# Attention inside a fused kernel, from the third batch on: four heads to a piece, score products on 64 array rows

## The chip, the cores and the metric

The kernel runs on one core of a Trainium2 chip. Its engines are TensorE (PE in the profile; PEld is its loading of stationary operands), VectorE (DVE), ScalarE (ACT), GpSimd (POOL) and the queue engine SyncE (SP). The metric is the device time of one execution in microseconds, lower is better.

## The reference

Masked attention over 8 batches, 8 heads, 576 positions and 64 values per head, followed by a gated two-layer network over all 4608 positions. All of it is float32.

```
scores = q @ k.T / sqrt(64)            # per batch and head
heads 0-3: keep 0 <= q_pos - k_pos < 32
heads 4-7: keep k_pos <= q_pos with k_pos % 32 == q_pos % 32
attn = softmax(where(kept, scores, -1e9));  x = attn @ v
x -> [4608, 512]                       # 8 heads side by side
h = x @ w_in                           # [512, 2048]
out = (h * erf(softplus(h))) @ w_out   # [2048, 512]
```

The masks are so sparse that a block of 96 (local heads) or 126 (strided heads, positions sorted by remainder) queries needs only 128 or 126 keys.

## The kernel before

**The network** is 192 slots: 12 chunks of 384 positions by 16 tiles of 128 hidden values. A slot is a first product `mm1` of 12 matmuls (line 457, tile `h` in PSUM, three buffers), a chain of ten steps that alternates between ACT and DVE and computes the gate (lines 465, 462, 492, 495, 498; the DVE step on line 492 is the last reader of `h` and so frees its buffer), and a second product `mm2` of nine matmuls (line 527) into three accumulators `o`. Each float32 factor is split into a high and a low part, hence three products each.

**Attention** works in pieces. A piece is one batch `b`, one pair of heads `hp` (0 and 1 local, 2 and 3 strided) and one third `j` of the positions. Local pieces have two blocks of 96 queries by two heads; strided ones two blocks of 126 (`j` 0 and 1) or one of 72 (`j` 2). The steps of a piece, for batches 2 to 7:

- `scores` on PE (line 261): per block one matmul. The stationary operand is 128 keys, with the 64 values of one head on array rows 0 to 63 and those of the other on rows 64 to 127. The moving operand is block diagonal: the queries of head 0 with zeros below, then those of head 1 with zeros above, so 192, 252 or 144 columns of which each is half zero.
- `mask` on DVE (line 282) adds the mask and moves the scores from PSUM to SBUF, `maxi` on POOL (line 287) takes the maximum over partitions, `sub` on DVE (line 296) subtracts it, `exp` on ACT (line 300).
- `av` on PE (line 304): per block and head one matmul with the probabilities as the stationary operand and 65 moving columns (the 65th of ones gives the sum). Then sum, reciprocal and scaling on DVE, `transp` on PE (line 335), and a split into `xhi` (ACT) and `xlo` (DVE), from which `mm1` reads.

A float32 matmul of the program appears as two weight loads and two matmul rows in the trace; a transpose as one.

Batches 0 and 1 run ahead of and into the first slots, with the mask added by PE. Attention for a later pair of batches runs among the slots of the pair before.

**What sets the order.** A planner (`Plan`) holds all steps with an assumed duration, a key and their inputs, and lays them out by list scheduling: on each engine, of what can start soonest, the lowest key. A step that opens a buffer waits until the last reader of the buffer it replaces. The result is written out engine by engine, and the engines run it in that order. Attention shares two PSUM buffers, `ps`, among score tiles, `av` tiles and transposes; SBUF buffers are two for `qk`, `mx`, `xn` and `r`, and three for `sm` and `v`.

Of the kernel before, what the change touches and what calls it, by code (L numbers as in the profile page):

```python
# [8 lines left out]
F32 = mybir.dt.float32  # L9
# [3 lines left out]
AF = mybir.ActivationFunctionType  # L13
ALU = mybir.AluOpType

B, H, S, D = 8, 8, 576, 64
DM, DF = 512, 2048
NT = B * S
P = 128
# [9 lines left out]
PRO, SLOT = 78.281, 5.385  # L29
# [4 lines left out]
A0K, A0S, A0D = 6.648, 4.179, -9.111  # L34
A1K, A1S, A1D = PRO - 0.655, 3.9, 5.799
ASH, ADT = -0.644, 1.759
# [3 lines left out]
QL = 96  # L40
RB = 7
NA = S // 32
QS = RB * NA
WL = 2 * 2 * QL + 2 * QL + 32
WS = 2 * 2 * QS + 2 * P
# [43 lines left out]
class Plan:  # L89
# [13 lines left out]
    def add(self, eng, dur, key, emit, after=(), new=(), use=(), earliest=0.0):  # L103
        op = Op(eng, dur, key, emit, after, new, use, earliest)
        self.ops.append(op)
        return op

    def _ready(self, op, live):
        t = op.earliest
        for p in op.after:  # L110
            if p.end is None:
                return None
            t = max(t, p.end + (self.SAME if p.eng == op.eng else self.LATENCY)[op.eng])
        for b in op.new:
            order = live.setdefault(b.tag, [])
            n = len(order) - self.bufs[b.tag]
            if n >= 0:
                for u in order[n].users:
                    if u.end is None:
                        return None  # L120
                    t = max(t, u.end + (self.SAME if u.eng == op.eng else self.LATENCY)[op.eng])
        return t
# [46 lines left out]
def attention_moe(  # L169
# [10 lines left out]
    nc = tc.nc  # L180
# [3 lines left out]
    apool = ctx.enter_context(tc.tile_pool(name="apool", bufs=2))  # L184
    mpool = ctx.enter_context(tc.tile_pool(name="mpool", bufs=2))
    wpool = ctx.enter_context(tc.tile_pool(name="wpool", bufs=1))
    ps_a = ctx.enter_context(tc.tile_pool(name="ps_a", bufs=2, space=PSUM))
# [3 lines left out]
    xhi = [cpool.tile([P, RING], F32R, name=f"xhi{c}") for c in range(NCC)]  # L191
    xlo = [cpool.tile([P, RING], F32R, name=f"xlo{c}") for c in range(NCC)]
    ident = cpool.tile([P, P], F32, name="ident")
    con = cpool.tile([P, NCON], BF16, name="con")
    mask_l = con[:, : 2 * QL].rearrange("p (b h q) -> p b h q", b=2, h=1)
    mask_s = con[:, 2 * QL : 2 * QL + QS].rearrange("p (u q) -> p u q", u=1)
# [7 lines left out]
    plan = Plan(bufs)  # L204
    pools = {"apool": apool, "mpool": mpool, "wpool": wpool, "ps_a": ps_a, "ps_h": ps_h, "ps_o": ps_o}

    def buf(pool, tag, shape, name, dtype=F32):
        def make():
            return pools[pool].tile(shape, dtype, tag=tag, name=name, bufs=bufs[tag])

        return Buf(tag, make)

    def dve(n, x=1.0):
        return 0.067 + n * x / 960.0

    def act(n, fixed=0.093):
        return fixed + n / 1200.0


    def piece(b, hp, j, key, dt, ring, pe_mask=False, pool_sub=False, early=False):  # L220
# [4 lines left out]
        loc = hp < 2  # L225
        nblk = 1 if (not loc and j == 2) else 2
        n = QL if loc else (QS if j < 2 else S - 4 * QS)
        units, cols = 2 * nblk, 2 * nblk * n
        pid = f"{b}_{hp}_{j}"
        qk = buf("apool", "qk", [P, WS], f"qk_{pid}")  # L230
        v = buf("apool", "v", [P, 2, 2, D + 1], f"v_{pid}")
        s = buf("ps_h", "h", [P, 512], f"s_{pid}") if early else buf("ps_a", "ps", [P, 512], f"s_{pid}")
        sm = buf("apool", "sm", [P, 4 * QS], f"sm_{pid}")
        mx = buf("apool", "mx", [P, 4 * QS], f"mx_{pid}")
        pav = buf("ps_o", f"o{hp % 2}", [P, 512], f"av_{pid}") if early else buf("ps_a", "ps", [P, 512], f"av_{pid}")
        xn = buf("apool", "xn", [P, 4, D], f"xn_{pid}")
        rc = buf("apool", "r", [P, 4, 1], f"r_{pid}")
        pt = buf("ps_a", "ps", [P, 512], f"t_{pid}")
# [121 lines left out]
        add = plan.add  # L360
        w = nblk * n
        lq = add("sp", P * 4 * (WL if loc else nblk * (2 * n + P)) / 3.6e5, key - 8.0, load_qk, new=[qk])
        lv = add("sp", P * 4 * nblk * 2 * (D + 1) / 3.6e5, key - 7.9, load_v, new=[v])
        per = max(2 * n / 600.0, 0.213) + (2 * n / 2400.0 if pe_mask else 0.0)
        o_s = add("pe", 0.02 + nblk * per, key, scores, [lq, *o_con], [s, sm], [qk])
# [11 lines left out]
        o_e = add("act", act(cols), key + dt + 0.1, exp, [o_b], [], [sm, s] if early else [sm])  # L377
        o_v = add("pe", 0.00174*n * units, key + dt + 0.2, av, [o_e, lv], [pav, xn], [sm, v])
        o_r = add("dve", 0.07, key + 1.5 * dt, total, [o_v], [rc], [pav])
        o_r = add("dve", 0.1, key + 1.5 * dt, invert, [o_r], [], [rc])  # L380
        if early:
            o_n = add("act", 0.2 * units, key + 1.5 * dt + 0.1, norm, [o_r], [], [pav, xn, rc])
        else:
            o_n = add("dve", dve(units * D), key + 1.5 * dt + 0.1, norm, [o_r], [], [pav, xn, rc])
        o_t = add("pe", 0.11 * nblk, key + 2 * dt, transp, [o_n] + ring, [pt], [xn])
        o_h = add("act", act(w, 0.06), key + 2 * dt + 0.1, split_hi, [o_t], [], [pt])
        return [add("dve", dve(w), key + 2 * dt + 0.2, split_lo_x, [o_h], [], [pt])]


    def weight(i, src, rows, sl, key):  # L390
# [175 lines left out]
    o = plan.add("sp", 0.6, -20.0, load_consts, new=[con_f])  # L566
    o_con = [plan.add("dve", 0.6, -19.0, copy_consts, [o], [], [con_f])]
# [3 lines left out]
    x_of = {}  # L571
# [3 lines left out]
    for f in range(0, DF, SW):  # L575
        for c in range(NCC):
            i = len(w1)
            rows, sl = slice(c * P, (c + 1) * P), slice(f, f + SW)
            op, pair = weight(i, w_in, rows, sl, W1K[i // 4] + W1S[i // 4] * (i % 4))
            w1.append(op)  # L580
            win.append(pair)
    for f in range(NFC):
        rows, sl = slice(f * P, (f + 1) * P), slice(0, DM)
        op, pair = weight(NFC + f, w_out, rows, sl, W2K + W2S * f)
# [3 lines left out]
    def order(b):  # L588
        if b % 2:
            return [(hp, j) for j in range(3) for hp in (0, 2, 1, 3)]  # L590
        if b == 0:
            return [(0, 0), (1, 0), (0, 1), (1, 1), (2, 0), (3, 0), (2, 1), (3, 1), (2, 2), (3, 2), (0, 2), (1, 2)]
        return [(hp, j) for j in range(2) for hp in range(2)] + [
            (2, 0), (3, 0), (0, 2), (2, 1), (3, 1), (1, 2), (2, 2), (3, 2)
        ]

    def chunk(c):
        need = [o for b in (2 * (c // 3), 2 * (c // 3) + 1) for o in x_of.get((b, c % 3), [])]
        for f in range(NFC):
            k = c * NFC + f  # L600
            ready = (need + w1[4 * (f // 4) : 4 * (f // 4) + 4], [w2[f]])
            mm1_of[k], _ = ftile(k, ready)
            mm1_first.append(mm1_of[k])

    for b in range(B):
        p2 = b // 2
        for i, (hp, j) in enumerate(order(b)):

            if b % 2 == 0:
                to = [0] if (hp < 2 and j < 2) else ([1] if hp < 2 else [0, 1])  # L610
            else:
                to = [1] if (hp < 2 and j == 0) else ([2] if hp < 2 else [1, 2])
            if b == 0:
                key, dt = A0K + A0S * i, A0D
            elif b == 1:
                key, dt = A1K + A1S * i, A1D
            else:
                if b % 2:
                    slot = 48 * p2 - 3 + (15 * i) / 11
                elif i < 4:  # L620
                    slot = 48 * (p2 - 1) + 13 + 4 * i
                else:
                    slot = 48 * (p2 - 1) + 29 + (15 * (i - 4)) / 7
                key, dt = PRO + SLOT * (slot + ASH), ADT * SLOT
            ring = []
            if p2:
                ring = [mm1_of[48 * (p2 - 1) + 16 * c + 15] for c in to]
            done = piece(b, hp, j, key, dt, ring, pe_mask=b < 2, pool_sub=False, early=b == 0)
            for c in to:
                x_of.setdefault((b, c), []).extend(done)  # L630
        if b % 2 == 0:
            continue
        for c in range(3 * p2, 3 * p2 + 3):
            chunk(c)
# [109 lines left out]
```

## Time and profile before

| | |
|---|---|
| median of 3 runs | 994.1 us (993.43 to 994.18) |
| profiled execution | 993.13 us |
| its span in the trace | 991.2 us |
| PE busy | 979.5 us, 99% of the span |
| DVE, ACT, POOL busy | 74%, 66%, 15% |

The span leaves 1.93 us of the execution outside the trace. The duration of a PE row covers a matmul from its first reading to its modelled end, and rows overlap; so what a stretch costs is read from the start of one row to the start of the next, which is what the chain of waits prints.

### The profile page before, as it was taken

What the parts mean: (1) busy time and instruction counts of PE and PEld (TensorE: products, weight loads), DVE (VectorE), ACT (ScalarE), POOL (GpSimd) and SP (SyncE); (2) the same over time, 40 slices, a digit from 0 to 9 for tenths busy, and PEclk for the clock granted to TensorE, in tenths of its full rate; (3) what the DMA queues carried; (4) which work ended last, traced back from release to release, by engine and by line L of the source; (5) the groups of instructions that cost most, each with busy time, mean ns of one, the idle gap of its engine ahead of it and who ended that gap; (6) DMA issues with size and microseconds to landing.
All of it is one profiled execution on the core that took longest, in us unless ns stands there. A gap on an engine that the chain in (4) does not pass through costs nothing.

```text
span 991.2 us, 15250 instructions
## 1 busy us (share of the span) xinstructions
PE 979.5 (99%) x5443; PEld 885.6 (89%) x5443; DVE 728.7 (74%) x1619; ACT 654.7 (66%) x1481; POOL 152.8 (15%) x100
## 2 busy tenths in 40 slices
PE   8999999999999999999999999999999999999998
PEld 6788999999899989999899999999899999999997
DVE  6999997677677776676777776776767776665664
ACT  4676777567566666666765665766766576766765
POOL 3534111111112110011112110111111210000000
PEclk9999999999999999999999999999999999999999
DMA  9994211111222211111222220211112220000000
GB/s 310 308 338 144 63 35 59 40 40 53 71 62 82 62 37 38 46 53 27 80 58 73 71 63 19 70 40 40 49 53 66 63 63 1 32 2 0 32 1 33
DMA packets 37659, 68.76 MB, mean 69 GB/s; under 512 B 4176, under 2 KB 18640, under 8 KB 37584
## 3 DMA queue, kind: packets, MB, share of 16 engines
q1 hardware_dynamic: 37584, 67.80, 22.1%
q8 instruction: 43, 0.70, 0.3%
q14 instruction: 32, 0.26, 0.1%
HBM read 58.34 MB, written 9.44 MB: 68 GB/s over the span
## 4 chain that ended last, share of the span: by engine, by line
PE 91%; DVE 8%; ACT 0%; issue 0%; DMA 0%
PE h L457 39%; PE o L527 39%; PE s L261 5%; PE av L304 5%; DVE w L415 1%; PE t L335 1%; DVE w L421 1%; DVE pair L429 1%; DVE a L462 1%; DVE w L408 1%; DVE glo L498 1%; DVE b L492 0%; DVE xlo L358 0%; DVE b L462 0%; PE warm L638 0%
## 5 line engine op out<-in xcount | busy, mean ns | idle before, releaser
L527 PE MATMUL o<-pair,ghi 128*128 128x512 f32 x1152 | 372.3, 404 | 0.0
L457 PE MATMUL h<-xhi,pair 128*128 128x384 f32 x1536 | 306.7, 341 | 1.4 <-DVE b L492 1.4
L457 PEld LDWEIGHTS h<-xhi,pair 128*128 128x128 f32 x1536 | 271.9, 188 | 15.7 <-DVE b L492 3.8
L465 ACT ACTIVATE b<-b 128x384 f32<-128x384 f32 x384 | 199.7, 521 | 104.2 <-DVE b L462 101.6
L287 POOL PARTITION_ALL_REDUCE mx<-sm x96 | 152.6, 1594 | 664.1 <-DVE sm L282 568.7
L527 PEld LDWEIGHTS o<-pair,ghi 128*128 128x128 f32 x1152 | 207.0, 188 | 28.0
L527 PE MATMUL o<-pair,glo 128*128 128x512 f32 x576 | 225.9, 392 | 0.0
L457 PE MATMUL h<-xlo,pair 128*128 128x384 f32 x768 | 165.9, 337 | 0.0
L498 DVE TENSOR_TENSOR glo<-b,ghi 128x384 fp32r<-128x384 f32 x192 | 110.5, 576 | 60.3 <-ACT ghi L495 59.8
L462 DVE SCALAR_TENSOR_TENSOR a<-h,a 128x384 f32<-128x384 f32 x192 | 106.4, 554 | 64.9 <-ACT a L465 63.3
L457 PEld LDWEIGHTS h<-xlo,pair 128*128 128x128 f32 x768 | 137.2, 187 | 0.0
L462 DVE SCALAR_TENSOR_TENSOR a<-a,h 128x384 f32<-128x384 f32 x192 | 105.5, 549 | 40.7 <-ACT b L465 38.6
L465 ACT ACTIVATE b<-a 128x384 f32<-128x384 f32 x192 | 100.5, 524 | 47.6 <-DVE glo L498 47.1
L527 PEld LDWEIGHTS o<-pair,glo 128*128 128x128 f32 x576 | 108.1, 188 | 24.1
L495 ACT CAST ghi<-b 128x384 fp32r<-128x384 f32 x192 | 97.9, 510 | 46.8 <-PE o L527 41.6
L492 DVE TENSOR_TENSOR b<-b,h 128x384 f32<-128x384 f32 x192 | 105.1, 547 | 31.2 <-ACT b L465 30.9
L465 ACT ACTIVATE a<-a 128x384 f32<-128x384 f32 x192 | 100.2, 522 | 26.6 <-DVE a L462 24.3
L465 ACT ACTIVATE a<-h 128x384 f32<-128x384 f32 x192 | 92.7, 483 | 33.4 <-PE h L457 32.3
L462 DVE SCALAR_TENSOR_TENSOR b<-b,a 128x384 f32<-128x384 f32 x192 | 110.5, 576 | 3.2
L304 PEld LDWEIGHTS av<-v,sm 128*96 128x96 f32 (+2 forms) x704 | 78.0, 171 | 7.8 <-ACT sm L300 1.5
L261 PE MATMUL s<-qk 128*128 128x192 f32 (+2 forms) x352 | 83.4, 351 | 0.1
L304 PE MATMUL av<-v,sm 128*96 128x65 f32 (+2 forms) x704 | 77.9, 251 | 1.1 <-ACT sm L279 0.7
(34 smaller groups left out, 588.4 us busy)
## 6 DMA issues: line engine op xcount, KB each, us to landing
qk<-qk_loc SPq DMA_DIRECT2D x48, 304.0 KB, 2.8
qk<-qk_str SPq DMA_DIRECT2D x32, 380.0 KB, 3.2
v<-v_all SPq DMA_DIRECT2D x80, 130.0 KB, 2.1
out<-ob SPq DMA_DIRECT2D x36, 256.0 KB, 2.1
words<-w_in SPq DMA_DIRECT2D x16, 512.0 KB, 5.6
words<-w_out SPq DMA_DIRECT2D x16, 512.0 KB, 5.9
qk<-qk_str SPq DMA_DIRECT2D x16, 136.0 KB, 2.1
v<-v_all SPq DMA_DIRECT2D x16, 65.0 KB, 1.9
```

Source lines behind the costliest of these rows:

```text
L261: yield nc.tensor.matmul(dst, qk[:, k0 + blk * step : k0 + blk * step + P], qk[:, blk * 2 * n : (blk + 1) * 2 * n], start=blk == 0, stop=n ...
L287: yield nc.gpsimd.partition_all_reduce(mx[:, :cols], sm[:, :cols], P, ReduceOp.max)
L304: yield nc.tensor.matmul(pav[:n, u * (D + 1) : (u + 1) * (D + 1)], sm[:, u * n : (u + 1) * n], v[:, u // 2, u % 2, :], start=True, stop=True,)
L335: yield nc.tensor.transpose(pt[:, blk * n : (blk + 1) * n], xn[:n, 2 * blk : 2 * blk + 2, :].rearrange("p h d -> p (h d)"), ident[:n, :n],)
L408: yield nc.vector.tensor_scalar(out=w.tile.bitcast(U32), in0=words[:, :, 1], scalar1=0x07FFFFFF, scalar2=3, op0=ALU.bitwise_and, op1=ALU.l ...
L457: yield nc.tensor.matmul(ph[:, :CH], win[4 * s + cc][:, w, fs], x[cc][:, c0 : c0 + CH], start=(i == 0), stop=(i == len(terms) - 1))
L462: yield nc.vector.scalar_tensor_tensor(out=out, in0=in0, scalar=scalar, in1=in1, op0=op0, op1=op1)
L465: yield nc.scalar.activation(dst, src, func, bias=bias[i], scale=scale)
L492: yield nc.vector.tensor_tensor(out=bb.tile, in0=bb.tile, in1=ph[:, :CH], op=ALU.mult)
L495: yield nc.scalar.copy(ghi.tile, bb.tile)
L498: yield nc.vector.tensor_tensor(out=glo.tile, in0=bb.tile, in1=ghi.tile.bitcast(F32), op=ALU.subtract)
L527: yield nc.tensor.matmul(po.tile, g[:, ts], wout[f][:, w], start=(f == 0 and i == 0), stop=(f == NFC - 1 and i == 2),)
```

## The change

From batch 2 on, `quad` takes the place of `piece`: both head pairs of a kind (hp 0 and 1, or 2 and 3) go through one set of steps. Six quads make a batch instead of twelve pieces. Of the planner, one line changes: a step that opens several buffers of one kind now waits for the last reader of as many old ones.

- `scores`: for two-block quads (`tiled`) the matmul of a block falls into one per head, each with 64 array rows and 96 or 126 moving columns without the zeros. All eight of a quad stand together; head 0 of each block goes to PSUM tile `s0`, head 1 to `s1`. The quad with one block keeps the block-diagonal form, four heads in one tile.
- `mask`, `maxi`, `sub`, `exp` work tile by tile: two of each per two-block quad, with as many columns as before (384 or 504); one of each with 288 columns for the one-block quad.
- `av` is one step of 16 (or 4) matmuls after both `exp`; transposes of both pairs go to one PSUM tile; the splits are unchanged.
- A two-block quad opens two `ps` tiles for scores and then two for `av`, so all that there are, and two of three `sm` buffers.

```diff
+        def place(i, blk, h):
+            if tiled:
+                return h, (2 * i + blk) * n
...
+        def scores():
+            k0, step = units * n, n if loc else P
+            used = set()
+            for i in range(2):
+                for blk in range(nblk):
+                    keys = slice(k0 + blk * step, k0 + blk * step + P)
+                    for h in range(2) if tiled else (slice(0, 2),):
+                        rows = slice(h * D, (h + 1) * D) if tiled else slice(0, P)
+                        bank, c = place(i, blk, h if tiled else 0)
+                        q0 = (blk * 2 + (h if tiled else 0)) * n
+                        width = n if tiled else 2 * n
+                        yield nc.tensor.matmul(
+                            s[bank][:, c : c + width], qk[i][rows, keys], qk[i][rows, q0 : q0 + width],
+                            start=bank not in used,
+                            stop=True, skip_group_check=True,
+                        )
+                        used.add(bank)
...
+        o_s = add("pe", d_s, key, scores, [*lq, *o_con], [*s, *sm], [*qk])
+        o_e = []
+        for k in range(nbank):
+            o = add("dve", dve(cols), key + 0.1 + 0.01 * k, mask(k), [o_s], [], [s[k], sm[k]])
+            o = add("pool", 0.4 + cols * 0.0028, key + 0.2 + 0.01 * k, maxi(k), [o], [mx[k]], [sm[k]], earliest=6.7)
+            o = add("dve", dve(cols), key + dt + 0.01 * k, sub(k), [o], [], [mx[k], sm[k]])
+            o_e.append(add("act", act(cols), key + dt + 0.1 + 0.01 * k, exp(k), [o], [], [sm[k]]))
+        o_v = add("pe", 0.00174 * n * 2 * units + 0.05, key + dt + 0.2, av, [*o_e, *lv], [*pav, *xn], [*sm, *v])
...
+                slot = 48 * p2 - 3 + 3 * i if b % 2 else 48 * (p2 - 1) + (13 + 8 * i if i < 2 else 29 + 4 * (i - 2))
...
+                done = quad(b, loc, j, PRO + SLOT * (slot + ASH), ADT * SLOT, ring)
```

On PE, the score product of the first strided piece of batch 4 stood in one place, and that of its sister in another, 25 rows later (`s` are score tiles, `o` the accumulators of `mm2`, `h` those of `mm1`; before, a name shows the head pair and the third):

```order
L335 MATMUL t_1_1_4736<-ident,xn_1_1_4650 128x96 x2
L261 MATMUL s_2_0_4740<-qk_2_0_4383 128x252 x2
L527 MATMUL o_4_4540<-pair_1162,ghi_4657 128x512 x2
...
L527 MATMUL o_4_4552<-pair_1267,glo_4719 128x512
L261 MATMUL s_3_0_4806<-qk_3_0_4572 128x252 x2
L457 MATMUL h_4814<-xhi_76,pair_646 128x384
```

Now the two stand together, as eight products of half the columns that change the score tile, and with it the half of the array, at each:

```order
L717 MATMUL o_4_4596<-pair_1049,glo_4648 128x512
L452 MATMUL s_4_2_0_4756<-qk_4_2_0_4407 128x126
L452 MATMUL s_4_2_0_4757<-qk_4_2_0_4407 128x126
L452 MATMUL s_4_2_0_4756<-qk_4_2_0_4407 128x126
L452 MATMUL s_4_2_0_4757<-qk_4_2_0_4407 128x126
L452 MATMUL s_4_2_0_4756<-qk_4_2_0_4414 128x126
L452 MATMUL s_4_2_0_4757<-qk_4_2_0_4414 128x126
L452 MATMUL s_4_2_0_4756<-qk_4_2_0_4414 128x126
L452 MATMUL s_4_2_0_4757<-qk_4_2_0_4414 128x126
L717 MATMUL o_4_4562<-pair_1162,ghi_4683 128x512 x2
```

Two places of PE at which it turns from the network to scores became one. On DVE, the mask of the same piece stood by itself between steps of the gate (`sm<-s,con` is the mask, `b<-b,h` the gate's product that frees an `h` buffer):

```order
L498 TENSOR_TENSOR glo_4748<-b_4673,ghi_4744 128x384
L282 TENSOR_TENSOR sm_2_0_4741<-s_2_0_4740,con 128x504
L358 TENSOR_TENSOR xlo_81<-t_1_1_4736,xhi_77 128x192
L462 SCALAR_TENSOR_TENSOR a_4697<-a_4697,h_4677 128x384
L462 SCALAR_TENSOR_TENSOR b_4757<-b_4757,a_4697 128x384
L296 TENSOR_TENSOR sm_2_0_4741<-sm_2_0_4741,mx_2_0_4774 128x504
```

Now two masks stand in a row, ahead of such a product:

```order
L688 TENSOR_TENSOR glo_4771<-b_4689,ghi_4768 128x384
L468 TENSOR_TENSOR sm_4_2_0_4758<-s_4_2_0_4756,con 128x504
L468 TENSOR_TENSOR sm_4_2_0_4759<-s_4_2_0_4757,con 128x504
L682 TENSOR_TENSOR b_4753<-b_4753,h_4670 128x384
L652 SCALAR_TENSOR_TENSOR a_4720<-a_4720,h_4699 128x384
```

The number of masks on DVE is the same, but the product waits behind two of them and not one.

## Rows read from the trace of the kernel before

**Rows 1.** The page: busy time, share of the span, instructions
```profile
PE 979.5 (99%) x5443; PEld 885.6 (89%) x5443; DVE 728.7 (74%) x1619; ACT 654.7 (66%) x1481; POOL 152.8 (15%) x100
```

**Rows 2.** The page: shares of the chain that ended last
```profile
PE 91%; DVE 8%; ACT 0%; issue 0%; DMA 0%
```

**Rows 3.** Waits of PE from 100 us on
```profile
PE h L457 <- DVE b L492: 0.7, 3, 0.2
```

**Rows 4.** Busy time by stretch: PE, PEld, DVE, ACT, POOL, granted clock, DMA
```profile
260.00:500.00 240.00, 239.55 (x1328) 218.49 (x1328) 172.77 (x389) 156.56 (x351) 36.10 (x25) 1.00 0.19 55
```

**Rows 5.** Chain of waits, 240 to 430 us: start, us on the chain, step
```profile
248.46 0.24 PE s L261 x2
...
291.65 0.65 PE s L261 x4
292.30 0.83 PE av L304 x8
...
392.10 0.65 PE av L304 x8
392.75 2.17 PE h L457 x12
394.93 1.36 PE o L527 x6
396.29 2.12 PE h L457 x12
...
400.46 0.17 PE t L335 x2
400.62 0.68 PE s L261 x4
401.30 1.38 PE o L527 x6
...
425.95 0.85 PE s L261 x4
```

**Rows 6.** PE matmuls by form: busy, mean ns of one, idle before
```profile
L261 PE MATMUL s<-qk 128*128 128x192 f32 x192 | 43.1, 343 | 0.1
L261 PE MATMUL s<-qk 128*128 128x252 f32 x128 | 33.6, 378 | 0.0
```

**Rows 7.** PE weight loads by form
```profile
L457 PEld LDWEIGHTS h<-xhi,pair 128*128 128x128 f32 x1536 | 271.9, 188 | 15.7 <-DVE b L492 3.8
L261 PEld LDWEIGHTS s<-qk 128*128 128x128 f32 x352 | 60.7, 193 | 9.0 <-issue 1.9 <-DMA qk<-qk_loc 0.6
```

**Rows 8.** DVE from 95 us on, by form
```profile
L492 DVE TENSOR_TENSOR b<-b,h 128x384 f32<-128x384 f32 x166 | 90.9, 548 | 24.5 <-ACT b L465 24.2
L282 DVE TENSOR_TENSOR sm<-s,con 128x384 f32<-128x384 f32 x36 | 19.9, 554 | 8.1 <-PE s L261 8.1
L282 DVE TENSOR_TENSOR sm<-s,con 128x504 f32<-128x504 f32 x24 | 16.3, 680 | 3.5 <-PE s L261 3.2
L282 DVE TENSOR_TENSOR sm<-s,con 128x144 f32<-128x144 f32 x12 | 3.6, 303 | 1.4 <-PE s L261 1.4
```

**Rows 9.** Timeline around the first of the three waits of PE
```profile
261.65 0.55 DVE L492 TENSOR_TENSOR b<-b,h 128x384 f32<-128x384 f32 x1
262.25 1.50 PE L457 MATMUL h<-xhi,pair 128*128 128x384 f32 x7 [0.22 <-DVE b L492]
```

**Rows 10.** Timeline of POOL, one strided maximum
```profile
760.48 1.76 POOL L287 PARTITION_ALL_REDUCE mx<-sm  x1 [6.30 <-DVE sm L282]
```

**Rows 11.** The page: DMA issues, KB each, us to landing
```profile
qk<-qk_str SPq DMA_DIRECT2D x16, 136.0 KB, 2.1
```

More of the change, by code (lines that the diff above doesn't have):

```diff
@@ L113, in _ready @@
             t = max(t, p.end + (self.SAME if p.eng == op.eng else self.LATENCY)[op.eng])
-        for b in op.new:
+        for i, b in enumerate(op.new):
             order = live.setdefault(b.tag, [])
-            n = len(order) - self.bufs[b.tag]
+            n = len(order) - self.bufs[b.tag] + sum(x.tag == b.tag for x in op.new[:i])
             if n >= 0:
@@ L211, in buf, with named @@
         return Buf(tag, make)
+    def named(name, f):
+        f.__name__ = name
+        return f
     def dve(n, x=1.0):
@@ L387, in piece, with quad, load_qk, load @@
         return [add("dve", dve(w), key + 2 * dt + 0.2, split_lo_x, [o_h], [], [pt])]
+    def quad(b, loc, j, key, dt, ring):
+        hps = (0, 1) if loc else (2, 3)
+        nblk = 1 if (not loc and j == 2) else 2
+        n = QL if loc else (QS if j < 2 else S - 4 * QS)
+        units, w = 2 * nblk, nblk * n
+        tiled = nblk == 2
+        nbank = 2 if nblk == 2 else 1
+        cols = 4 * w // nbank
+        pid = f"{b}_{hps[0]}_{j}"
+        qk = [buf("apool", "qk", [P, WS], f"qk{i}_{pid}") for i in range(2)]
+        v = [buf("apool", "v", [P, 2, 2, D + 1], f"v{i}_{pid}") for i in range(2)]
+        s = [buf("ps_a", "ps", [P, 512], f"s{i}_{pid}") for i in range(nbank)]
+        sm = [buf("apool", "sm", [P, 4 * QS], f"sm{i}_{pid}") for i in range(nbank)]
+        mx = [buf("apool", "mx", [P, 4 * QS], f"mx{i}_{pid}") for i in range(nbank)]
+        pav = [buf("ps_a", "ps", [P, 512], f"av{i}_{pid}") for i in range(2)]
+        xn = [buf("apool", "xn", [P, 4, D], f"xn{i}_{pid}") for i in range(2)]
+        rc = [buf("apool", "r", [P, 4, 1], f"r{i}_{pid}") for i in range(2)]
+        pt = buf("ps_a", "ps", [P, 512], f"t_{pid}")
+        def place(i, blk, h):
+            if tiled:
+                return h, (2 * i + blk) * n
+            c = (blk * 2 + h) * n
+            return (i, c) if nbank == 2 else (0, i * 2 * w + c)
+        def load_qk(i):
+            def load():
+                if loc:
+                    yield nc.sync.dma_start(qk[i][:, :WL], qk_loc[b, hps[i], j])
+                else:
+                    cw = nblk * (2 * n + P)
+                    yield nc.sync.dma_start(qk[i][:, :cw], qk_str[b, hps[i] - 2, j, :, :cw])
+            return load
+        def load_v(i):
+            def load():
+                cw = nblk * 2 * (D + 1)
+                yield nc.sync.dma_start(
+                    v[i].tile.rearrange("p b h d -> p (b h d)")[:, :cw], v_all[b, hps[i], j, :, :cw]
+                )
+            return load
+        def scores():
[13 more added lines that the diff above has]
+                            stop=True, skip_group_check=True,
+                        )
+                        used.add(bank)
+        def mask(k):
+            def run():
+                src, dst = s[k][:, :cols], sm[k][:, :cols]
+                if loc:
+                    m = (mask_l if j == 0 else mask_l[:, 1:2]).rearrange("p b h q -> p h b q")
+                    r, z, m = "p (i b q) -> p i b q", dict(i=2, b=2), m.broadcast_to([P, 2, 2, n])
+                else:
+                    r, z = "p (u q) -> p u q", dict(u=cols // n)
+                    m = mask_s[:, :, :n].broadcast_to([P, cols // n, n])
+                yield nc.vector.tensor_tensor(
+                    out=dst.rearrange(r, **z), in0=src.rearrange(r, **z), in1=m, op=ALU.add
+                )
+            return named("mask", run)
+        def maxi(k):
+            def run():
+                yield nc.gpsimd.partition_all_reduce(mx[k][:, :cols], sm[k][:, :cols], P, ReduceOp.max)
+            return named("maxi", run)
+        def sub(k):
+            def run():
+                d = sm[k][:, :cols]
+                yield nc.vector.tensor_tensor(out=d, in0=d, in1=mx[k][:, :cols], op=ALU.subtract)
+            return named("sub", run)
+        def exp(k):
+            def run():
+                d = sm[k][:, :cols]
+                yield nc.scalar.activation(d, d, AF.Exp, scale=1.0 / D**0.5)
+            return named("exp", run)
+        def av():
+            for i in range(2):
+                for u in range(units):
+                    bank, c = place(i, u // 2, u % 2)
+                    yield nc.tensor.matmul(
+                        pav[i][:n, u * (D + 1) : (u + 1) * (D + 1)],
+                        sm[bank][:, c : c + n],
+                        v[i][:, u // 2, u % 2, :],
+                        start=True,
+                        stop=True,
+                    )
+        def norm(i):
+            a, rr = lambda: pav[i][:n, : units * (D + 1)].rearrange("p (u d) -> p u d", u=units), lambda: rc[i][:n, :units]
+            def total():
+                yield nc.vector.tensor_scalar(
+                    out=rr(), in0=a()[:, :, D : D + 1], scalar1=1e-9, scalar2=None, op0=ALU.add
+                )
+            def invert():
+                yield nc.vector.reciprocal(rr(), rr())
+            def scale():
+                yield nc.vector.tensor_tensor(
+                    out=xn[i][:n, :units], in0=a()[:, :, :D], in1=rr().broadcast_to([n, units, D]), op=ALU.mult
+                )
+            return total, invert, scale
+        def transp():
+            for i in range(2):
+                for blk in range(nblk):
+                    c = i * w + blk * n
+                    yield nc.tensor.transpose(
+                        pt[:, c : c + n], xn[i][:n, 2 * blk : 2 * blk + 2, :].rearrange("p h d -> p (h d)"), ident[:n, :n]
+                    )
+        def views(i, t):
+            base, src = (b % 2) * S, pt[:, i * w : (i + 1) * w]
+            if loc:
+                c0 = base + j * 2 * QL
+                return src, t[:, c0 : c0 + w]
+            r0 = 2 * RB * j
+            dst = t[:, base : base + S].rearrange("p (a r) -> p a r", r=32)[:, :, r0 : r0 + w // NA]
+            return src.rearrange("p (r a) -> p a r", a=NA), dst
+        def split(i):
+            def split_hi():
+                src, hi = views(i, xhi[hps[i]])
+                yield nc.scalar.copy(hi, src)
+            def split_lo_x():
+                src, hi = views(i, xhi[hps[i]].bitcast(F32))
+                _, lo = views(i, xlo[hps[i]])
+                yield nc.vector.tensor_tensor(out=lo, in0=src, in1=hi, op=ALU.subtract)
+            return split_hi, split_lo_x
+        add = plan.add
+        lq = [add("sp", P * 4 * (WL if loc else nblk * (2 * n + P)) / 3.6e5, key - 8.0 + 0.1 * i, load_qk(i), new=[qk[i]]) for i in range(2)]
+        lv = [add("sp", P * 4 * nblk * 2 * (D + 1) / 3.6e5, key - 7.8 + 0.1 * i, load_v(i), new=[v[i]]) for i in range(2)]
+        d_s = 1.27 if tiled else 2 * nblk * max(2 * n / 600.0, 0.213)
+        o_s = add("pe", d_s, key, scores, [*lq, *o_con], [*s, *sm], [*qk])
[6 more added lines that the diff above has]
+        o_v = add("pe", 0.00174 * n * 2 * units + 0.05, key + dt + 0.2, av, [*o_e, *lv], [*pav, *xn], [*sm, *v])
+        o_n = []
+        for i in range(2):
+            total, invert, scale = norm(i)
+            o = add("dve", 0.07, key + 1.5 * dt, total, [o_v], [rc[i]], [pav[i]])
+            o = add("dve", 0.1, key + 1.5 * dt, invert, [o], [], [rc[i]])
+            o_n.append(add("dve", dve(units * D), key + 1.5 * dt + 0.1, scale, [o], [], [pav[i], rc[i], xn[i]]))
+        o_t = add("pe", 0.09 + 0.11 * 2 * nblk, key + 2 * dt, transp, o_n + ring, [pt], [*xn])
+        done = []
+        for i in range(2):
+            hi, lo = split(i)
+            o = add("act", act(w, 0.06), key + 2 * dt + 0.1, hi, [o_t], [], [pt])
+            done.append(add("dve", dve(w), key + 2 * dt + 0.2, lo, [o], [], [pt]))
+        return done
@@ L603, in chunk, with pairs, chunks_of @@
             mm1_first.append(mm1_of[k])
+    def pairs(b):
+        if b % 2:
+            return [(True, 0), (False, 0), (True, 1), (False, 1), (True, 2), (False, 2)]
+        return [(True, 0), (True, 1), (False, 0), (True, 2), (False, 1), (False, 2)]
+    def chunks_of(b, loc, j):
+        if b % 2 == 0:
+            return [0] if (loc and j < 2) else ([1] if loc else [0, 1])
+        return [1] if (loc and j == 0) else ([2] if loc else [1, 2])
     for b in range(B):
         p2 = b // 2
[L607 to L626, printed above, removed]
+        if p2 == 0:
+            for i, (hp, j) in enumerate(order(b)):
+                to = chunks_of(b, hp < 2, j)
+                key, dt = (A0K + A0S * i, A0D) if b == 0 else (A1K + A1S * i, A1D)
+                done = piece(b, hp, j, key, dt, [], pe_mask=True, pool_sub=False, early=b == 0)
+                for c in to:
+                    x_of.setdefault((b, c), []).extend(done)
+        else:
+            for i, (loc, j) in enumerate(pairs(b)):
+                to = chunks_of(b, loc, j)
+                slot = 48 * p2 - 3 + 3 * i if b % 2 else 48 * (p2 - 1) + (13 + 8 * i if i < 2 else 29 + 4 * (i - 2))
                 ring = [mm1_of[48 * (p2 - 1) + 16 * c + 15] for c in to]
-            done = piece(b, hp, j, key, dt, ring, pe_mask=b < 2, pool_sub=False, early=b == 0)
-            for c in to:
-                x_of.setdefault((b, c), []).extend(done)
+                done = quad(b, loc, j, PRO + SLOT * (slot + ASH), ADT * SLOT, ring)
+                for c in to:
+                    x_of.setdefault((b, c), []).extend(done)
         if b % 2 == 0:
```

## The prediction

> **What bounds the kernel now.** I read the page's busy times first. PE is busy in 99% of the span, DVE in 74%, ACT in 66%, POOL in 15% [rows 1]. A busy PE alone proves little, since its rows overlap, so next come the shares of the chain that ended last: 91% PE, 8% DVE [rows 2]. Then the waits of PE once the weights are in: 0.7 us in three events of 0.2 us, all of `mm1` waiting for the gate's product on DVE [rows 3]. The table by stretch gives the same for 260 to 500 us: PE works in 239.55 of 240 us at a granted clock of 1.00, the 2.4 GHz level [rows 4]. So from the first slots on the kernel is a stream of matmuls without gaps. What a change takes out of this stream is gained, unless a new wait opens; what it does to DVE, ACT or POOL counts only where PE comes to wait for it.
>
> The chain of waits prices the stream, because there each step reaches to the start of the next [rows 5]. Of attention, a two-block score product costs 0.65 us (local, four rows of 192 columns) or 0.85 us (strided, 252); the small one 0.24 us; `av` 0.65 or 0.83 us for eight rows.
>
> **What one row costs.** Scores: 0.65 / 4 = 0.162 us for 192 columns and 0.85 / 4 = 0.212 us for 252, which is 0.84 ns a column both times. So these products are bound by their moving columns; half the columns would be 0.081 (96) and 0.106 us (126). `av` moves only 65 columns, and its price goes with the stationary operand: 0.65 / 8 = 0.081 us for 96 loaded columns, 0.83 / 8 = 0.104 us for 126, so 0.84 ns for each loaded column. There the load is the bound. Score loads have 128 columns, by the same rate 0.107 us (an estimate from these rows), and were hidden behind 0.162 and 0.212 us.
>
> **The change, part by part.** Batches 2 to 7 have 36 local, 24 large strided and 12 small pieces; they become 18, 12 and 6 quads. Batches 0 and 1 and the whole of the network keep their instructions.
>
> *Score products.* Before, a quad's worth cost 2 x 0.65 = 1.30 us local and 2 x 0.85 = 1.70 us strided. Now it is eight matmuls, so 16 loads and 16 rows, alternating between halves of the array after every second row. No row of before shows two halves at work, so I bound it.
> - Best: the halves work side by side, loads too. Then each half does eight rows at the pace of its load, 8 x 0.107, and with one step more to start, 9 x 0.107 = 0.96 us for either kind.
> - Worst: loads pass one at a time, 16 x 0.107 = 1.71 us, for either kind.
> - Between: loads overlap but rows run one after another, 16 x 0.081 = 1.30 us local and 16 x 0.106 = 1.70 us strided, just as before.
>
> *Going into halves and back.* PE may have to empty itself where it turns from full rows to half rows and again on the way back. No row shows such a turn. A score row lasts 343 ns while the next starts after 162 [rows 6], so emptying costs up to 0.18 us; and a load that no longer hides shows its 193 ns [rows 7], so up to 0.37 us a turn and 0.74 us a burst. From below it is nothing: between network and attention of full height turns cost some hundredths (below). I take 0.18 us a turn, the emptying with the load hidden, since loads of the network do hide: 188 ns each [rows 7], while `mm1` goes on at 2.12 / 12 = 0.177 us. So a burst is 0.96 + 0.36 = 1.32 us.
> The Trainium skill speaks against the change here: in "TensorEngine Tiling (Array Packing)", section Key Properties, it says that a change of tiling mode drains the engine, though not how long that takes. It also says there that tiles load and multiply in parallel, which is my first bound. No run so far shows either.
>
> The sum of these: local 1.32 − 1.30 = +0.02 us x 18 = +0.4 us; large strided 1.32 − 1.70 = −0.38 x 12 = −4.6 us. The small quad keeps its form: 2 x 0.24 before, the same four rows now, 0.
>
> *Fewer turns.* 72 score, 72 `av` and 72 transpose stretches become half as many. Around one, the neighbours are a little longer: `mm1` 2.17 us behind an `av` against 2.12 us elsewhere, `mm2` 1.38 behind scores against 1.36 [rows 5]. Between nothing and 0.05 us for each; I take 0.02 us for scores (with the 0.68 us that the same four rows cost in one place) and 0.04 us for `av`, none for transposes: 36 x 0.06 = −2.2 us.
>
> *`av` and transposes* keep their rows: 16 x 0.081 or 16 x 0.104 us, and four transposes at 0.17 / 2. Nothing.
>
> *Mask, subtraction, exponential.* As many of them with as many columns; only the small quad saves, one DVE step in two of 303 ns [rows 8]. But two stand in a row now: behind the second mask (554 or 680 ns [rows 8]) waits the gate's product, which frees the `h` buffer that a later `mm1` needs. That this wait can bite shows in the trace: DVE ends the product at 262.20 us and PE, idle for 0.22 us, starts `mm1` at 262.25 [rows 9]. In place of one such wait in each of three periods I allow two, so +0.7 us once more; its upper bound is a rival below.
>
> *POOL and the buffers.* The two maxima of a quad go one after the other, 1.76 us each for strided ones [rows 10], and `av` waits for both. From the end of the scores to `av` a strided quad so needs some 2 x 0.68 (mask, subtraction) + 2 x 1.76 + 0.63 (exponential, as a strided mask or less) = 5.5 us and half a microsecond of handing over, against 4 for a piece. In the new order the shortest stretches of PE work there, counted with the prices above, are about 6.5 us for a local quad, which needs some 0.8 us less, and 7.9 us for a strided one; that covers it with a microsecond to spare. Without that cover, what is missing adds to each quad. Two `ps` tiles per step mean that a quad's scores wait for the other quad's tiles; these are read within some 2 us after the burst, and other attention mostly comes later. DMA: the same 96 loads of `qk` and of `v`; but a quad takes both `qk` buffers, so that the next one's loads start only behind its burst. The tightest place is the small quad some 5 us behind the last local one of an odd batch, and its loads land after 2.1 us each [rows 11]. Nothing, and the missing part of those 5 us if the queue is late, in three places.
>
> **Sum:** +0.4 − 4.6 − 2.2 + 0.7 = −5.7 us. The profiled execution took 993.13 us (span 991.2 and 1.93 outside it), so 987.4 us; the median of the runs shown is 1.0 us above that execution, so 988.4 us.
>
> **Rivals.**
>
> A. *The turn costs nothing that shows.* Then a burst is 0.96 us: 18 x −0.34 = −6.1 and 12 x −0.74 = −8.9 us, with −2.2 + 0.7 in all −16.5 us, 977.6 us. For it: loads of the network hide fully even on rows that are in use [rows 7]. Against it: the slack of the `h` buffers is short [rows 3, 9], and DVE would have to follow a PE that is 2% faster.
> The Trainium skill, "TensorE: Matmul & The Clock Gate", section Measured speedup vs the span model, gives 3.07 times for four row tiles. If two gained in proportion, 1.5 times, bursts would be 0.85 and 1.11 us, near this rival's; no row here bears on it.
>
> B. *The loads pass one at a time* (slower). Mechanism: the change doubles the weight loads of the scores, from 8 to 16 a quad, and with 128 columns each they become the bound. `av` speaks for it: its rows come exactly as fast as loads can follow each other, none beside another [rows 5]. Against it: there every load covers the whole height of the array. Price: bursts of 1.71 us, local +0.41 x 18 = +7.4, strided 0, with −1.5 us from the rest 1000.0 us; with the turns (0.36 x 30 = 10.8 us) 1010.8 us. It decides as soon as a load takes more than 0.081 us that another half cannot use: then local quads lose.
>
> C. *The change doesn't do what it says:* halves run one after another, loads hidden. Bursts cost what they cost before, 994.1 − 1.5 = 992.6 us.
>
> D. *DVE in pairs* (slower). Place: the gate's product behind two masks, and again near the two subtractions. If `mm1` comes half a microsecond late for each of 30 two-block quads, +15 us on the forecast: 1003 us. It decides where the `h` buffer comes free less than one mask (0.55 us) before PE wants it. For it: [rows 9]. Against it: only 0.7 us of such waits in the whole trace [rows 3], and DVE has a quarter of its time free [rows 1].
>
> **How the numbers follow.** Forecast 0.44, with its own range 984 to 992 us (turns of 0.05 to 0.30 us; waits of nothing to 3 us). A 0.20, B 0.13, C 0.10, D 0.13. The range 977 to 1002 us leaves out half of A's lower side, B with its turns, and D's far end, together about 0.2. A measurement of this kernel can tell some 0.2%, 2 us, from no change, so faster means below 992.1 us: nearly all of the forecast (0.43), A and the mild ends of D (0.02), 0.65. Within it: C and an edge, 0.12. Slower: B and D with the worst edge, 0.23.
>
> **What would show it.** In the profile after: the chain's price of eight half-height products, 1.32 us by the forecast, 0.96 by A, 1.71 or more by B, 1.30 local and 1.70 strided by C. The turns show at the first `o` or `h` rows behind a burst and the last before it. Waits of PE for `b` on line 682 or for exponentials above 3 us in all would show D or a late chain. The forecast is wrong as a mechanism if local and strided bursts differ by more than 0.2 us, or if PE waits for more than it saves.

## The result, and the profile after

The changed kernel takes 984.16 us (median of 4 runs, 983.26 to 985.08) against 994.14 us in the same comparison: a ratio of 0.9897 (0.988 to 0.9914), 10.0 us less, where 5.7 us were forecast. The profiled execution has a span of 981.9 us, 9.3 us less than before.

The page after, its busy times and its chain shares, beside [rows 1, 2]:

```profile
PE 970.0 (99%) x5683; PEld 871.8 (89%) x5683; DVE 720.9 (73%) x1607; ACT 654.0 (67%) x1475; POOL 146.4 (15%) x94
...
PE 92%; DVE 6%; DMA 1%; issue 0%; ACT 0%; SPq 0%
```

PE has 240 rows more and is still busy for 99% of a shorter span. The table by stretch for the same 240 us as [rows 4]:

```profile
260.00:500.00 240.00, 240.00 (x1438) 217.21 (x1437) 170.91 (x390) 157.62 (x350) 35.70 (x24) 1.00 0.19 57
```

The clock is the same (1.00) and PE has no gap left. From 100 us on, where [rows 3] has three waits of PE, there is none; the last one of the trace stands before that, at an `av` of batch 0 or 1:

```profile
PE av L308 <- ACT sm L283: 0.7, 1, 0.7
```

The chain of waits of the changed kernel (start, us on the chain, step), for [rows 5], shows a quad's parts:

```profile
388.79 1.33 PE av L498 x16
...
398.51 0.33 PE t L528 x4
...
412.82 2.72 PE o L717 x12
415.54 1.09 PE s L452 x16
416.63 2.26 PE o L717 x9
...
421.01 2.04 PE o L717 x9
...
431.90 3.42 PE o L717 x15
435.32 1.07 PE s L452 x16
436.39 2.95 PE o L717 x12
```

The 16 rows of a burst take 1.09 us strided and 1.07 us local. What the burst costs reaches beyond them: nine `o` rows behind it take 2.26 instead of 2.04 us, twelve 2.95 instead of 2.72. So a burst is about 1.29 us, whichever kind it is. Counted from all row starts (a burst with the network row on either side, less 0.227 us for an `o` row and 0.1755 for an `h` row, which is what they take elsewhere) it is 1.27 us local and 1.29 us strided; two pieces of before, counted the same way, were 1.32 and 1.71 us.

The score rows by form, for [rows 6], and their loads, for [rows 7], of the changed kernel (from 100 us on for the loads):

```profile
L452 PE MATMUL s<-qk 64*128 64x96 f32 x288 | 20.4, 281 | 0.0
...
L452 PE MATMUL s<-qk 64*128 64x126 f32 x192 | 13.9, 284 | 0.0
```

```profile
L452 PEld LDWEIGHTS s<-qk 64*128 64x128 f32 x480 | 29.1, 187 | 8.6 <-issue 6.1 <-PE o L717 2.5
```

480 loads of 187 ns would fill 90 us one behind the other; their rows cover 29.1 us, so three are under way on average. Before, 352 full-height loads of 193 ns covered 60.7 us [rows 7]. The starts of the rows of a burst lie 7, 105, 7, 105 ns apart and so on: two rows start almost together, and a pair follows the last after 112 ns (the second pair follows the first after 187 to 212). At 112 ns one behind the other, 480 loads would need 53.8 us.

Masks and subtractions of the changed kernel on DVE from 95 us on, for [rows 8]:

```profile
L682 DVE TENSOR_TENSOR b<-b,h 128x384 f32<-128x384 f32 x187 | 102.5, 548 | 44.3 <-ACT b L655 43.9
...
L483 DVE TENSOR_TENSOR sm<-sm,mx 128x384 f32<-128x384 f32 x36 | 23.9, 673 | 3.3 <-POOL mx L476 3.2
...
L468 DVE TENSOR_TENSOR sm<-s,con 128x384 f32<-128x384 f32 x36 | 18.7, 552 | 0.7 <-PE s L452 0.7
```

The mask and the gate's product cost what they did (the counts of [rows 8] end at 900 us; over the same time as here there were 187 products before, too). The subtraction does not, on which more below.

The start of the span differs by up to 3.3 us among the profiled executions, one of each kernel: without batch 1 in quads, the thirteenth `mm1` starts between 115.85 and 119.16 us. So the experiments also give the stretch from the start of the thirteenth `mm1` (at 116.08 us before, 116.25 after) to the start of the last matmul (986.82 and 977.75): 870.7 us before and 861.5 after, 9.2 us less. The rows of PE in it are the same but for a few that stand on the other side of its start: the two kernels of pieces have three `o` rows and a transpose more and four score rows fewer, together 0.1 us.

### The profile page after: what moved, and what is told of

Read it like the earlier page. It is cut to its first block, busy times and chain, and to the rows that moved or that the text cites. A ratio compares the mean times of both kernels' runs of the same rounds, so it can differ in the third digit from the quotient of the medians.

```text
span 981.9 us, 15767 instructions
## 1 busy us (share of the span) xinstructions
PE 970.0 (99%) x5683; PEld 871.8 (89%) x5683; DVE 720.9 (73%) x1607; ACT 654.0 (67%) x1475; POOL 146.4 (15%) x94
## 4 chain that ended last, share of the span: by engine, by line
PE 92%; DVE 6%; DMA 1%; issue 0%; ACT 0%; SPq 0%
PE h L647 40%; PE o L717 40%; PE av L498 5%; PE s L452 4%; DVE w L605 1%; DVE w L611 1%; PE t L528 1%; DVE pair L619 1%; DVE w L598 1%; PE s L265 1%; DMA words<-w_in 1%; PE av L308 1%; DVE xlo L362 0%; DVE a L652 0%; DMA qk<-qk_loc 0%; DVE b L652 0%
## 5 line engine op out<-in xcount | busy, mean ns | idle before, releaser
L717 PE MATMUL o<-pair,ghi 128*128 128x512 f32 x1152 | 364.2, 397 | 0.0
L476 POOL PARTITION_ALL_REDUCE mx<-sm x66 | 101.2, 1572 | 599.4 <-DVE sm L468 599.4
L688 DVE TENSOR_TENSOR glo<-b,ghi 128x384 fp32r<-128x384 f32 x192 | 110.5, 576 | 60.7 <-ACT ghi L685 51.2
L498 PEld LDWEIGHTS av<-v,sm 128*96 128x96 f32 (+2 forms) x528 | 54.2, 172 | 2.2
L291 POOL PARTITION_ALL_REDUCE mx<-sm x24 | 45.1, 1890 | 64.2 <-ACT sm L283 58.6
L498 PE MATMUL av<-v,sm 128*96 128x65 f32 (+2 forms) x528 | 53.3, 253 | 0.0
```

The lines of the kernel that those rows point to most:

```text
L291: yield nc.gpsimd.partition_all_reduce(mx[:, :cols], sm[:, :cols], P, ReduceOp.max)
L476: yield nc.gpsimd.partition_all_reduce(mx[k][:, :cols], sm[k][:, :cols], P, ReduceOp.max)
L498: yield nc.tensor.matmul(pav[i][:n, u * (D + 1) : (u + 1) * (D + 1)], sm[bank][:, c : c + n], v[i][:, u // 2, u % 2, :], start=True, stop= ...
L688: yield nc.vector.tensor_tensor(out=glo.tile, in0=bb.tile, in1=ghi.tile.bitcast(F32), op=ALU.subtract)
L717: yield nc.tensor.matmul(po.tile, g[:, ts], wout[f][:, w], start=(f == 0 and i == 0), stop=(f == NFC - 1 and i == 2),)
```

## The experiments

| kernel | median us | ratio to before | thirteenth `mm1` to end, us |
|---|---|---|---|
| before | 994.1 | | 870.7 |
| pieces in the quads' slots | 993.0 | 0.9988 (0.9979 to 0.9997) | 869.4 |
| quads, full height | 990.7 | 0.9965 (0.9952 to 0.9977) | 866.9 |
| **changed kernel** | 984.2 | 0.9897 (0.988 to 0.9914) | 861.5 |
| half 0, then half 1 | 999.5 | 1.0054 (1.0039 to 1.007) | 877.2 |
| a turn inside the burst | 992.9 | 0.9987 (0.9978 to 0.9996) | 870.2 |
| small quads in halves | 988.1 | 0.9932 (0.9918 to 0.9946) | 863.1 |
| batch 1 in quads | 996.6 | 1.0024 (1.0014 to 1.0033) | |

The ratios are to the kernel before as it ran beside each, at a median of 994.1 or 994.2 us every time. The interval of each ratio is in brackets.

**Full height in quads.** Everything of the change but the 64-row products.

```diff
-        tiled = nblk == 2
+        tiled = False
...
```

The lines left out fit the mask to the other order of columns and keep the planner's assumed duration of a burst.

> The quads stay, in the same order on every engine, but their score products go back to full height: per block one matmul of 192 or 252 block-diagonal columns, both pairs still in one burst. Theory 'two halves at once': a burst costs 1.27 us (local) and 1.29 us (strided) in the changed kernel, counted from the trace as what it adds to the neighbours, and 1.32 and 1.71 us for the two pieces before; so this run gives back 18 x 0.05 + 12 x 0.42 = 5.9 us and takes about 990.1 us, with bursts of 1.30 and 1.70 us. Theory 'regrouping': the gain comes from fewer turns and from waits that went, and the short rows only look parallel: within 1.5 us of 984.2 us.

It took 990.7 us, 6.5 us more than the changed kernel (5.4 us in the stretch). Its chain of waits:

```profile
415.62 2.73 PE o L717 x12
418.35 1.70 PE s L452 x8
420.06 2.05 PE o L717 x9
...
435.03 3.42 PE o L717 x15
438.45 1.30 PE s L452 x8
439.75 2.75 PE o L717 x12
```

The bursts are 1.70 and 1.30 us, and the `o` rows behind them are nearly as short as elsewhere (2.05 and 2.75 us against 2.04 and 2.72): at their ends full-height scores cost hundredths of a microsecond. Against 1.29 and 1.27 us that is 12 x 0.41 + 18 x 0.03 = 5.5 us. The theory of two halves at once holds; regrouping alone accounts for the other 3.4 us (994.1 to 990.7).

**Half by half.** The eight products of a burst in another order.

```diff
-            for i in range(2):
-                for blk in range(nblk):
...
-                    for h in range(2) if tiled else (slice(0, 2),):
+            for h in range(2) if tiled else (slice(0, 2),):
+                for i in range(2):
+                    for blk in range(nblk):
...
```

> The same eight half-height products of a burst, but all four of array half 0 first and then all four of half 1. Theory 'two halves at once': rows overlap only where the half changes; within a half they follow at the pace of the load, 0.105 to 0.112 us, so 16 rows take about 1.75 us and the turns 0.37 us: bursts of 2.1 us, +0.85 us x 30 = +25 us, 1009 us. Rival 'short rows are simply cheap' (loads pass in pairs whatever the half): bursts stay at 1.27 us, 984 us.

999.5 us: 15.3 us more than the changed kernel (15.7 in the stretch), not 25 and not nothing. The chain of waits, and the loads of the scores from 100 us on:

```profile
418.57 2.72 PE o L717 x12
421.29 1.64 PE s L452 x16
422.93 2.27 PE o L717 x9
...
438.12 3.42 PE o L717 x15
441.55 1.59 PE s L452 x16
443.13 2.96 PE o L717 x12
```

```profile
L452 PEld LDWEIGHTS s<-qk 64*128 64x128 f32 x480 | 45.0, 187 | 8.6 <-issue 6.1 <-PE o L717 2.5
```

A burst costs 1.78 or 1.84 us by the count with neighbours, half a microsecond more, and 30 of them make 15.9 us. Within a half rows follow singly after 112 ns, as expected; so the pairs of the changed kernel are rows of different halves. What I had missed is the middle: there the starts lie 6, 106, 81, 30, 81, 31, 81 ns apart (local), so that the loads of half 1 had gone ahead of the last rows of half 0, and three or four rows of each half still ran side by side. So the gain hangs on work for both halves being near each other in the order. Fewer columns alone gain nothing: 1.78 and 1.84 us are more than the 1.30 and 1.70 at full height.

**A turn inside the burst.**

```diff
             for i in range(2):
+                if tiled and i:
+                    yield nc.tensor.matmul(
+                        s[0][:, 504:512], ident_b, con[:, :8], start=False, stop=True, skip_group_check=True
+                    )
```

> In the middle of each of the 30 half-height bursts one full-height matmul of 8 columns is added, into unused columns of the score tile. Theory 'a turn costs': going from half height to full and back adds what the two ends of a burst add now, 1.27 - 8 x 0.112 = 0.37 us, plus some 0.03 us for the matmul: 30 x 0.40 = +12 us, 996 us. Rival 'the ends are only pipeline filling that any change of operands would cost': 0.03 to 0.08 us each, +1 to +2.5 us, 985 to 987 us.

992.9 us, 8.7 us more (8.7 in the stretch as well), so 0.29 us for each added pair of turns, the added row included: between the two, and nearer to the first. The chain of waits:

```profile
416.86 2.72 PE o L721 x12
419.57 0.64 PE s L456 x8
420.22 0.11 PE s L446
420.33 0.64 PE s L456 x8
420.97 2.27 PE o L721 x9
```

Eight half-height rows take 0.64 us where a middle pair costs 0.112: the first and the last of each run are slow, and so is the one row of 8 columns between them (0.11 us). The added row is in bfloat16 while its neighbours are float32, but that change of type is at most a small part of the price: in batches 0 and 1 full-height bfloat16 rows stand between float32 rows of scores, and the float32 row behind one takes 0.19 us to the next start instead of 0.16 (192 columns). A turn is a price of its own. It is 0.29 us for two here and 0.37 us (1.27 − 8 x 0.112) at the ends of a burst, where long rows stand beside it.

**Pieces in the quads' slots.** The kernel before, with both pieces of a kind given the slot of the quad.

```diff
-                if b % 2:
-                    slot = 48 * p2 - 3 + (15 * i) / 11
...
+                i //= 2
+                slot = 48 * p2 - 3 + 3 * i if b % 2 else 48 * (p2 - 1) + (13 + 8 * i if i < 2 else 29 + 4 * (i - 2))
```

> The kernel before, with its pieces of two heads and full-height products, but both pieces of a kind at the time slots that the quads have. Theory 'the waits went with the slots': PE loses the three waits for the gate's product (0.7 us, some 2 us with the slower rows around them) and a few turns, but keeps its score rows: 991 to 992.5 us. Rival 'they went with the steps of four heads' (one av, one burst, no second piece between): no change against 994.1 us within 1 us, or slower, since two pieces in a row compete for two PSUM buffers.

993.0 us, 1.1 us less than before (1.4 in the stretch): between the two theories. The waits of PE's loads for the gate's product from 100 us on, in four kernels: before, pieces in the quads' slots, quads at full height, changed.

```profile
PEld h L457 <- DVE b L492: 2.8, 6, 0.7
```

```profile
PEld h L457 <- DVE b L492: 3.2, 10, 0.5
```

```profile
PEld h L647 <- DVE b L682: 0.3, 1, 0.3
```

```profile
PEld h L647 <- DVE b L682: 0.7, 3, 0.3
```

New slots spread these waits over more places but leave their sum (2.8 to 3.2 us). Only the quads make them go (0.3 and 0.7).

What the waits cost PE itself can be counted from row starts. Where an `mm1` follows an `mm2`, its first row starts 0.227 us after the last `o` row unless it has to wait; what goes beyond that adds up to 1.7 us in the stretch before (of which three times 0.39 us at 262, 500 and 737 us), 1.0 us for pieces in the quads' slots, and 0.1 and 0.2 us for the two kernels with quads. So of the 1.5 us that these waits gave back, 0.6 came with the new slots and 0.9 with the steps of four heads.

The same starts give the turns from the network to attention. PE makes 166 of them in the stretch before, 131 with pieces in the quads' slots, since only some pairs come to stand together there, and 106 with quads at either height. So this run's 1.4 us are 0.6 us of waits, and 0.8 us are left for 35 turns; the full-height quads' 3.8 us are 1.5 us of waits, and 2.3 us are left for 60 turns. That the rest is turns is a subtraction, not a measurement.

What made PE wait before shows in its chain ahead of the first of the three waits:

```profile
255.74 0.31 DVE sm L282
...
256.81 0.29 DVE xn L329
...
258.49 0.54 DVE sm L282
...
261.74 0.48 DVE b L492
...
262.25 2.38 PE h L457 x12
```

For 6.5 us the chain runs mostly over DVE, where two masks and the scaling of attention stand between steps of the gate. In the chain of the changed kernel these microseconds are PE alone. Why a quad's steps leave the gate's product more room on DVE, though its masks stand in pairs, no run took apart; that stays open.

**Small quads in halves.** Four products of 72 columns in place of two of 144, in two tiles.

```diff
-        tiled = nblk == 2
-        nbank = 2 if nblk == 2 else 1
+        tiled = True
+        nbank = 2
...
-                return h, (2 * i + blk) * n
+                return h, (nblk * i + blk) * n
...
```

> The changed kernel with the six one-block quads in half-height products too: four products of 72 columns, 8 rows, in place of two of 144. Theory 'a burst is 0.37 us for its two turns plus 0.112 us for each pair of rows': 0.37 + 4 x 0.112 = 0.82 us against 0.50 us now, so +0.32 x 6 = +1.9 us, 986 us; short bursts lose. Rival 'half height always pays when columns are cut' (no fixed price): 4 x 0.112 = 0.45 us, no change, 984 us.

The median is 988.1 us, 3.9 us above the changed kernel, with runs from 985.55 to 988.92. The stretch grows by 1.6 us, and the rest lies before it, where this profiled execution was 2.9 us late already. The small burst in its chain, between network rows:

```profile
246.05 2.08 PE o L717 x9
248.13 0.60 PE s L452 x8
248.72 2.95 PE o L717 x12
```

0.60 us and again 0.23 us behind it (twelve `o` rows are 2.72 us elsewhere), against 0.50 us for four full rows in the changed kernel. By the count with neighbours it is 0.80 us against 0.50; six of them are 1.8 us, where the sum of turns and pairs gave 1.9 and the stretch 1.6. And with 72, 96 and 126 columns the pairs keep their 112 ns: moving columns do not set that pace.

**Batch 1 in quads.** The try at a version that beats both.

```diff
+            for i, (loc, j) in enumerate(pairs(b) if b else []):
+                to = chunks_of(b, loc, j)
+                done = quad(b, loc, j, A1K + A1S * (2 * i + 0.5), A1D, [])
...
+            for i, (hp, j) in enumerate(order(b) if b == 0 else []):
```

> The changed kernel with batch 1 in quads as well (its mask then added by DVE instead of by 22 bfloat16 matmuls on PE). Theory 'PE still bounds the first slots': per batch the bursts save 3 x 0.05 + 2 x 0.42 = 1.0 us, the 22 mask products go (0.08 to 0.11 us each, 2.0 us), turns some 0.3 us: -3.3 us, 981 us. Rival 'DVE bounds the first slots' (it is busy in nine tenths of the stretch from 50 to 120 us, where weights are unpacked, and gets twelve mask steps of 0.55 to 0.68 us more): no gain or slower, 984 to 988 us.

996.6 us, 12.4 us slower than the changed kernel. The loss lies in the first slots: the thirteenth `mm1` starts at 129.3 us instead of 116.2. The waits of PE in this kernel, its stretch from 50 to 100 us, and the timeline at one of the waits:

```profile
PE h L647 <- DVE b L682: 4.8, 3, 2.0
PE av L498 <- ACT sm L490: 4.0, 3, 2.4
```

```profile
50.00:100.00 50.00, 43.76 (x268) 38.84 (x267) 46.53 (x105) 31.04 (x74) 14.71 (x7) 0.90 0.63 222
```

```profile
61.35 1.01 DVE L468 TENSOR_TENSOR sm<-s,con 128x384 f32<-128x384 f32 x2
...
62.28 0.54 DVE L682 TENSOR_TENSOR b<-b,h 128x384 f32<-128x384 f32 x1
...
62.88 1.99 PE L647 MATMUL h<-xhi,pair 128*128 128x384 f32 x8 [1.81 <-DVE b L682]
```

The rival holds, and more. Where weights are still unpacked, PE does not bound. Here the wait behind two masks, which the prediction feared for batches 2 to 7 (its rival D), does bite: they hold DVE until the gate's product starts at 62.28 us, and PE has been idle for 1.81 us when `mm1` starts. Mask, maximum and subtraction of two tiles in a row make `av` late as well (4.0 us in three waits). After the longest of these gaps the granted clock falls to its lower level, 1.2 GHz, for a while: in this stretch it is 0.90 on average where the changed kernel has 1.00.

Both halves of the array writing into one PSUM tile at the same time was not tried, so whether the two banks are needed stays open.

## Why the prediction was right, and where its sizes were off

- *What bounds the kernel* was right: what left the stream of matmuls came off the time.
- *The burst* was right as a mechanism and nearly in size: 1.32 us forecast, 1.27 and 1.29 measured, so nearly the same for both kinds. Two halves load and multiply side by side at the pace of the load: 112 ns a pair, estimated as 107 from `av`. The two errors in it are small and opposite: the pairs were taken 5 ns too short, and what comes on top of eight pairs (a starting step of 0.107 us and 0.36 us for the turns, 0.47 in all) measured 0.37 to 0.39. By the Trainium skill, "TensorEngine Tiling (Array Packing)", section Key Properties, a change of tiling mode drains the engine, and tiles load and multiply in parallel. The traces agree with both: an added pair of turns costs 0.29 us, and two rows take 112 ns. Strided quads gave 12 x 0.42 = 5.0 us (4.6 forecast), and local ones 18 x 0.05 = 0.9 us, where a loss of 0.4 was forecast. Undoing it alone cost 5.4 us in the stretch and 6.5 us in the medians; 4.2 were forecast.
- *Rival A* fell: a burst costs 1.27 and 1.29 us and not 0.96, and a second pair of turns in each costs 8.7 us. *Rival B* fell: a burst is far from 1.71 us, and 480 loads cover 29.1 us. *Rival C* fell: a strided burst costs 1.29 us where the same scores at full height cost 1.70. The 1.5 times that I had taken in proportion from a measured speedup in the Trainium skill ("TensorE: Matmul & The Clock Gate", section Measured speedup vs the span model) was an estimate for bursts of 0.85 and 1.11 us; measured are 1.27 and 1.29.
- *Fewer turns* was put at −2.2 us, and 2.3 us are left for them in the full-height quads. The sum is right; how it splits among scores, `av` and transposes, of which the forecast gave the last nothing, no run shows.
- *The added wait* is the step that failed, in sign: "+0.7 us once more" came out as −1.5. From 100 us on PE no longer waits for the gate's product, where it waited three times before, and the loads' waits for it fell from 2.8 to 0.7 us. The term was also read too small: the view counts 0.2 us of idle time for each of the three waits, while by row starts `mm1` came 0.39 us late. Rival D, the same step at its upper bound, fell with it. I had read that two masks stand ahead of one product, and not asked how often a product would find any mask ahead of it; whether that is the reason isn't shown.

In the stretch, 5.4 us for the half-height products, 2.3 for turns and 1.5 for waits make the 9.2 us, where 4.2 + 2.2 − 0.7 = 5.7 were forecast. Of the 3.5 us between them the wait has 2.2 and the bursts 1.2. The medians lie 0.7 us further apart than the stretches; the runs do not show where that comes from. So the direction and the main mechanism were right. Both misses went the same way, and the time came in at the lower edge of the forecast's own range, 984 to 992 us.

## What to carry to other kernels

A matmul that fills half the array's rows with zeros can be split into two that use the halves together, if products for both halves alternate and each burst is long enough to pay for its two turns (here 0.3 to 0.4 us: eight products of 126 columns gained 0.4 us a burst, eight of 96 hardly anything, and four of 72 lost 0.3). Such a burst goes at the pace of its weight loads, so it pays most where moving columns were the bound. Group small steps of different shape on a full engine, but look first at which engine bounds the stage: the same grouping cost 12 us where PE was not the bound.

## What the runs showed of the hardware that was not expected

Loads for the other half run ahead even when all its products stand behind those of the first half: in the half-by-half run the first row of half 1 starts 6 ns after the fifth of the eight rows of half 0.

A subtraction on DVE that starts while POOL takes a maximum can wait for it. In the changed kernel, where a quad's second maximum follows its first, the form 128x384 rose from 550 ns on average before to 673 (line L483 above), and the longest subtraction is 1.51 us. The timeline of the changed kernel around it, POOL and DVE:

```profile
460.73 3.51 POOL L476 PARTITION_ALL_REDUCE mx<-sm  x2 [20.75 <-DVE sm L468]
...
462.52 1.51 DVE L483 TENSOR_TENSOR sm<-sm,mx 128x504 f32<-128x504 f32 x1 [0.36 <-POOL mx L476]
...
465.92 0.68 DVE L483 TENSOR_TENSOR sm<-sm,mx 128x504 f32<-128x504 f32 x1
```

The two maxima run from 460.73 to 464.24 us (spans on POOL are rough), the first subtraction from 462.52 to 464.03; the second, with no maximum beside it, takes 0.68 us. This fits the Trainium skill, "SBUF — State Buffer", section Who interferes with whom, by which a VectorE instruction with two SBUF inputs contends with a GpSimd one that reads SBUF. In the changed kernel PE has no wait from 100 us on, so it cost PE nothing there.
